# An RWKV-7 block and its experts: k and b side by side in one tile, their products with v and U joined, the slots in another order

## The chip, the cores and the metric

The kernel runs on one core of a Trainium2 chip. The metric is device time in microseconds (us); lower is better. PE is the matrix engine (its weight loads are shown apart, as PEld), DVE the vector engine, ACT the scalar engine, POOL GpSimd, SP the engine that issues most DMAs. "L371" is line 371 of the kernel before.

## What is computed

Sizes: B = 4 batches, H = 8 heads, S = 768 steps, D = 40; then N = 3072 tokens of 320, E = 8 experts of 1024, capacity 80. All float32.

```python
state = zeros(B, H, D, D)
for t in range(S):
    y[:, :, t] = einsum('bhd,bhde->bhe', r_t, state)
    Sa = einsum('bhde,bhe->bhd', state, a_t)
    state = state * w_t[:, :, None, :] - outer(Sa, b_t) + outer(v_t, k_t)
x = y.transpose(0, 2, 1, 3).reshape(B * S, H * D)
logits = x @ w_gate                      # argmax expert, its softmax weight
for e in range(E):                       # at most 80 tokens, by largest weight
    out[tok] = weight[tok, None] * (relu(x[tok] @ w1[e]) @ w2[e])
```

## The kernel before, in words

**Tiling.** The sequence is cut into 12 chunks of T = 64 steps, the batches into two pairs (BP = 2, Z = 2 batches in each), which gives 24 units, in the order chunk 0 pair 0, chunk 0 pair 1, chunk 1 pair 0 and so on. A unit holds 2 batches x 8 heads x 64 steps; partitions are 2 x 64 steps, or, turned, two heads (parity q) x 64 with 40 used. Unit n needs the state that unit n - 2 left.

**What a unit needs.** Within a chunk the recurrence becomes matrix products. decays (L241) turns w with PE transposes and products (L246) takes running products pt with a scan on DVE. decayed_a (L251) makes ahT. inverted (L257) turns pt back with PE, takes its reciprocal on DVE (L265), and POOL multiplies b and k by it (L267, L268) into ub and kh. operand_b and system (L271, L274) turn ub and form the scores N with ahT; the blocks of N go to DRAM. operand_k and psi (L317, L320) do the same for kh: Psi, masked by POOL (L227).

**The inversion.** Four units make a group (NG = 4). fetch (L286) reads the group's 32x32 blocks back, one block per partition; begin (L290) masks them on POOL; 30 steps (L297) of two DVE products each invert the blocks; end (L308) writes them to DRAM and reads them back as dt. Unit n = 4k needs group k's dt.

**A unit's own slot.** right (L343): a first part of PE products from psi and v, a second from the state's copy state_b and ahT; diagonal, below, diagonal (L366, L358) apply the inverse and give u. Then, one slot later (o = n - 1): turned, rT and vT (L382, L327), lower (L391: two sets of scores, copied to lam and masked by POOL), rows (L398, from the turned state gT of reads_g, L332), summed (L409: products with kh and ub), xT and acc on DVE, the new state on POOL (L427), spread (L375: ACT copies the state to state_b). logits (L431) turns xT, writes rows to DRAM and sums the gate's logits; per group, gate (L450) makes weights and keeps running lists of the largest 80 by 10 rounds (L490, L491) on DVE.

**What sets the order.** The order is written out by hand in the loop of L582, and do (L510) chains the instructions of PE, DVE, ACT and POOL in exactly that order; SP's follow their own. Inversion steps and rounds wait in one list, todo; pause(us) (L531) takes from it until the stated costs are used up. PSUM tiles of transposes and small products share the pool ps_t, three buffers (L143); scores have one (L144). Inputs have two buffers each and are loaded two units ahead. Seven units are prepared before the loop (AHEAD = 7, L138), the first inversion among them.

**The end.** The lists are merged, a table of tokens per expert is made, and eight experts are computed; their weights are loaded once the first phase has ended (L648).

Of the kernel before, what the change touches and what calls it, by code (L numbers as in the profile page):

```python
# [18 lines left out]
def kernel(  # L19
# [49 lines left out]

    NF = DM // 128  # L70
    XW = 2 * DM - NF * 128
    assert DM - NF * 128 == 64
    FK = F // 128

    x_dram = nc.dram_tensor("x_rows", (N, XW), F32, kind="Internal")

# [59 lines left out]
    with ExitStack() as p1:  # L136
# [5 lines left out]
        sb = p1.enter_context(tc.tile_pool(name="sb", bufs=2))  # L142
# [8 lines left out]
        def padded(name, n, shape, fill=0.0, where=lambda t: t):  # L151
# [7 lines left out]
        def dims(t):  # L159
            return t[:, :, D:HB]  # L160

        NK = AHEAD + 3
        raw = {n: padded(f"raw_{n}", 2, [128, H, HB], 1.0 if n == "w" else 0.0, dims) for n in inputs}
        decay = padded("decay", 2, [128, G, Z, T + 1], 0.0, lambda t: t[:, :, :, 0:1])
        ubs = padded("ub", NK, [128, H, HB], 0.0, dims)
        khs = padded("kh", NK, [128, H, HB], 0.0, dims)
        us = padded("u", 2, [128, H, HB], 0.0, dims)

        state = padded("state", BP, [128, Z, G, HB], 0.0, lambda t: t)
        state_b = padded("state_b", BP, [128, Z, G, 2, D])  # L170
        og_t = padded("og", 2, [128, NG, 32])
        cand = padded("cand", 2, [128, capr + ZT])

        (lam,) = [hold.tile([128, 2, 2, G, T + D], F32, name="lam")]
# [5 lines left out]
        def load(n, names, queues=(nc.sync, nc.sync)):  # L180
            if n >= NU:
                return
            c, bp = units[n]
            for name in names:
                for z in range(Z):
                    queues[z].dma_start(raw[name][n % 2][halves[z], :, 0:D],
                                        inputs[name][Z * bp + z, :, c * T : (c + 1) * T, :].rearrange("h t d -> t h d"))
# [17 lines left out]
        def copied(name, t, bufs=2):  # L205
            o = sb.tile([128, G, 128], F32, name=name, tag=name, bufs=bufs)
            nc.scalar.copy(o, transposed(t))  # L207
            return o
# [3 lines left out]
        def scores(lhs, rhs):  # L212

            p = ps_s.tile([128, 2, 512], F32, name="sp", tag="s")
            p = p.rearrange("p q (i g t) -> p q i g t", i=2, g=G)
# [14 lines left out]
        def block(z, i):  # L230
            return slice(z * T + i * C, z * T + (i + 1) * C)
# [350 lines left out]
        for n in range(NU + 2):  # L582
# [8 lines left out]
            if past:  # L591
                do(beside, o)
# [242 lines left out]
```

## Time and the profile before

| | |
|---|---|
| median of 3 runs | 674.28 us (668.98 to 681.53) |
| the profiled execution's own time | 669.64 us |
| its span, first to last instruction | 667.9 us |
| mean granted PE clock | 0.912 |
| busy: PE, PEld, DVE, ACT, POOL | 500.3, 434.3, 368.1, 239.0, 197.3 us |
| DMA packets | 224900, of which 205333 under 512 B |
| first copy of a slot (L356) begins | 108.0 us |
| last xT (L421) begins | 537.1 us |

The page gives busy times and what idle time an engine had before a group of instructions, with the one that ended it. It has 40 slices of the span, in which a digit is the busy share in tenths; PEclk is the clock that PE was granted. A timeline row is a run of like instructions: start, length, engine, line, operation, tile written and tiles read, shapes, count. PE executes a float32 product as two instructions, so 16 products are 32 rows' counts; a transpose is one. The loop's slots can be cut at the starts of L356.

### The profile page before, as it was taken

The numbers are of one execution on the slowest core, as the hardware profiler recorded it, in microseconds if no ns is written. First come the engines' busy times: TensorE is split into PE (matmuls) and PEld (weight loads), VectorE is DVE, ScalarE is ACT, GpSimd is POOL, SyncE is SP. The second block draws the span as 40 slices with busy tenths as digits, with TensorE's granted clock in tenths as the row PEclk, the third lists the DMA queues.
The fourth block names the chain that finished last, engine by engine and source line by source line (L and its number), as shares of the span: only waits on it lengthen the run. The fifth ranks groups of instructions, "written<-read, shape, count | busy, mean of one in ns | idle before, by whom it ended". The sixth has DMA issues, their size and how long they took to land. (4 is left out here: it accounts for less than half of the span.)

```text
span 667.9 us, 25885 instructions
## 1 busy us (share of the span) xinstructions
PE 500.3 (75%) x11494; PEld 434.3 (65%) x11494; DVE 368.1 (55%) x851; ACT 239.0 (36%) x500; POOL 197.3 (30%) x273
## 2 busy tenths in 40 slices
PE   3755048798958798886997799769799721799996
PEld 2544037688847688875887688758688620677774
DVE  7525952795349964897659961885150058401110
ACT  1221014455625545553564535554545400000000
POOL 4222012425424424532444433422222200112111
PEclk9999999979978989987998989998989855599999
DMA  8653366535665466545553143123211008999200
GB/s 109 101 108 42 62 117 116 80 60 136 126 149 105 70 149 140 112 94 112 99 115 69 36 97 75 34 75 58 50 19 37 15 12 275 358 318 325 68 7 19
DMA packets 224900, 69.29 MB, mean 104 GB/s; under 512 B 205333, under 2 KB 219797, under 8 KB 224789
## 3 DMA queue, kind: packets, MB, share of 16 engines
q1 hardware_dynamic: 217344, 64.85, 44.1%
q10 hardware_dynamic: 6676, 0.99, 1.1%
q8 instruction: 90, 1.47, 1.0%
q0 software_dynamic: 768, 1.80, 0.9%
q14 instruction: 22, 0.17, 0.1%
HBM read 51.85 MB, written 15.76 MB: 101 GB/s over the span
## 5 line engine op out<-in xcount | busy, mean ns | idle before, releaser
L303 DVE TENSOR_TENSOR tmp<-tt,lt 128x30 f32<-128x30 f32 (+9 forms) x180 | 75.5, 420 | 25.3 <-POOL tt L292 20.5
L306 DVE TENSOR_TENSOR tt<-tt,tmp 128x30 f32<-128x30 f32 (+9 forms) x180 | 79.3, 441 | 6.6
L267 POOL TENSOR_TENSOR ub<-raw_b,ip 128x320 f32<-128x320 f32 x24 | 21.5, 894 | 200.3 <-DVE ip L265 179.6
L227 POOL TENSOR_SCALAR_AFFINE_SELECT lam<-lam 64x1024 f32<-64x1024 f32 x48 | 56.1, 1168 | 71.0 <-ACT lam L395 69.1
L265 DVE RECIPROCAL ip<-pp 128x320 f32<-128x320 f32 x24 | 51.7, 2155 | 37.1 <-PE pp L262 37.1
L421 DVE TENSOR_TENSOR xT<-yp,pt 128x512 f32<-128x512 f32 x24 | 16.5, 687 | 72.8 <-PE yp L417 72.7
L785 ACT ACTIVATE hT<-hp 128x320 f32<-128x320 f32 x16 | 6.1, 434 | 108.7 <-PE hp L781 108.7
L249 DVE TENSOR_TENSOR_SCAN pt<-decay,begins 128x520 f32<-128x520 f32 x24 | 30.0, 1248 | 26.5 <-ACT decay L243 26.5
L262 PE MATMUL pp<-pick,pt 128*64 128x80 f32 x384 | 22.3, 271 | 29.0 <-DVE pt L249 29.0
L417 PE MATMUL yp<-lam,kh 64*64 64x104 f32 (+1 forms) x768 | 29.6, 261 | 16.5 <-POOL lam L227 16.2
L793 DVE TENSOR_SCALAR y<-yp,weight 80x320 f32<-80x320 f32 x8 | 4.4, 547 | 67.6 <-PE yp L791 67.6
L262 PEld LDWEIGHTS pp<-pick,pt 128*64 128x64 f32 x384 | 18.9, 166 | 32.1 <-issue 26.2
L227 POOL TENSOR_SCALAR_AFFINE_SELECT psi<-psi 64x512 f32<-64x512 f32 x48 | 32.2, 672 | 20.2 <-ACT psi L324 18.6
L791 PE MATMUL yp<-w,hT 128*80 128x320 f32 x128 | 37.0, 436 | 0.0
L371 PE MATMUL pr<-yy,dt 32*32 32x40 f32 x1536 | 36.6, 199 | 0.2 <-ACT yy L364 0.2
L371 PEld LDWEIGHTS pr<-yy,dt 32*32 32x32 f32 x1536 | 30.8, 107 | 8.4 <-issue 6.5
L406 PE MATMUL yp<-rT,gT 64*64 64x64 f32 x768 | 35.9, 260 | 0.0
L417 PEld LDWEIGHTS yp<-lam,kh 64*64 64x64 f32 x768 | 22.0, 140 | 21.2 <-POOL lam L227 21.2
L406 PEld LDWEIGHTS yp<-rT,gT 64*64 64x64 f32 x768 | 32.1, 170 | 4.4 <-issue 3.9
L207 ACT COPY ubT<-tp 128x512 f32<-128x512 f32 x24 | 14.1, 586 | 58.1 <-PE tp L202 58.0
L427 POOL TENSOR_TENSOR state<-acc,pt 128x320 f32<-128x320 f32 x22 | 25.0, 1135 | 32.1 <-DVE acc L426 25.1
L395 ACT COPY lam<-sp 128x512 f32<-128x512 f32 x48 | 25.8, 589 | 16.8 <-PE sp L220 16.8
(343 smaller groups left out, 1159.1 us busy)
## 6 DMA issues: line engine op xcount, KB each, us to landing
w<-in_moe_w_dram SPq DMA_DIRECT2D x8, 1280.0 KB, 14.9
w<-in_moe_w_dram SPq DMA_DIRECT2D x8, 1024.0 KB, 16.6
x_rows<-xb SPq DMA_DIRECT2D x48, 96.0 KB, 2.6
out_dram<-zero SPq DMA_DIRECT2D x8, 480.0 KB, 3.6
raw_w<-in_w_dram SPq DMA_DIRECT2D x46, 80.0 KB, 3.0
raw_a<-in_a_dram SPq DMA_DIRECT2D x46, 80.0 KB, 2.8
raw_b<-in_b_dram SPq DMA_DIRECT2D x46, 80.0 KB, 3.0
raw_k<-in_k_dram SPq DMA_DIRECT2D x46, 80.0 KB, 2.9
```

The source lines that it names most:

```text
L227: nc.gpsimd.affine_select(out=oo, in_=oo, compare_op=Alu.is_gt, fill=0.0, base=0, pattern=[[0, oo.shape[1]], [1, T]], channel_multiplier=-1)
L249: nc.vector.tensor_tensor_scan(flat(pt), flat(decay[n % 2]), flat(begins), 0.0, op0=Alu.mult, op1=Alu.add)
L262: nc.tensor.matmul(p[halves[z], g, :], lhsT=pt[:, g, z, 1:], rhs=pick[:, 0, 0 : 2 * D], start=g == 0, stop=True, skip_group_check=True)
L265: nc.vector.reciprocal(ip, p.rearrange("p g (q d) -> p (g q) d", q=2))
L303: nc.vector.tensor_tensor(out=tm, in0=t3[:, 0:i, i : i + 1].to_broadcast([128, i, n]), in1=l3[:, i : i + 1, i + 1 :].to_broadcast([128, i, ...
L306: nc.vector.tensor_tensor(out=t3[:, 0:i, i + 1 :], in0=t3[:, 0:i, i + 1 :], in1=tm, op=Alu.add)
L371: nc.tensor.matmul(o["pr"][m, h, :], lhsT=dt_[m, n % NG, h % 2, h // 2, :], rhs=o["yy"][m, h, :], start=h == 0, stop=True, skip_group_chec ...
L395: nc.scalar.copy(lam[:, :, q, :, 0:T], p[:, q])
L406: nc.tensor.matmul(y[m, z, g, 0:T], lhsT=o["gT"][m, z, g, :], rhs=o["rT"][m, g, halves[z]], start=g == 0, stop=False, skip_group_check=True)
L417: nc.tensor.matmul(o["y"][m, z, g, 0:w_], lhsT=x[halves[z], 2 * g + q, :], rhs=lam[halves[z], i, q, g, 0:w_], start=False, stop=i == 1, sk ...
L427: nc.gpsimd.tensor_tensor(out=st[:, :, :, 0:D], in0=acc, in1=o["pt"][:, :, :, T : T + 1].rearrange("p g z o -> p z g o").to_broadcast([128 ...
L791: nc.tensor.matmul(yp, lhsT=hT[:, f, :], rhs=w2[:, f, :], start=f == 0, stop=f == FK - 1)
```

## The change

- k and b of a batch are loaded onto the two halves of one tile (raw_s): batch 0 has k in partitions 0 to 63 and b in 64 to 127, batch 1 the other way. scaled holds both after the multiplication by inverse decays; u lies beside v in the same manner (side).
- The inverse decays come from a scan backward (backward: a reciprocal of each chunk's last product, then products from the end), not from L265; DVE multiplies (inverted), not POOL.
- operand turns both at once, system forms N and Psi in one set of products whose left side has 128 columns; one copy (system_kept) keeps both, and POOL masks them. lower does the same for v and u. summed has one product where there were two, over all 128 partitions. gT is block diagonal, and rows uses it whole.
- N goes to DRAM whole, in 2 KB rows; fetch takes 32x32 blocks from it with four DMAs.
- Inputs and most tiles of the pool sb have one buffer; SP is chained in order too.
- The loop's order is new. Steps and rounds have lists of their own, with other costs and pauses. x_rows holds 320 values per token, and tokens makes the doubled last 64 with two products.

Its core (turned and system keep their names; `...` marks what is left out):

```diff
-        sb = p1.enter_context(tc.tile_pool(name="sb", bufs=2))
+        sb = p1.enter_context(tc.tile_pool(name="sb", bufs=1))
...
+        raw = {n: filled(f"raw_{n}", i, [128, H, HB], 1.0 if n == "w" else 0.0, lambda t: t[:, :, D:])
+               for n, i in (("w", 1), ("a", 1), ("r", 1))}
...
+        scaled = filled("scaled", NK, [128, Z, H, HB], 0.0, lambda t: t[:, :, :, D:])
+        side = hold.tile([128, 1 + SLOTS, Z, H, HB], F32, name="side")
+        nc.gpsimd.memset(side[:, 1:], 0.0)
...
+        (gT,) = filled("gT", 1, [128, Z, G, 2, HB])
...
+        def by_half(t):
+            ps = [ps_t.tile([128, Z, G, T], F32, name="tp", tag="t") for _ in range(2)]
+            for z in range(Z):
+                for g in range(G):
+                    for p, m in zip(ps, halves):
+                        nc.tensor.transpose(p[:, z, g, :], t[m, z, 2 * g : 2 * g + 2, :].rearrange("p q d -> p (q d)"), ident[m, m])
...
-                            nc.tensor.matmul(p[z, q, i, g, :], lhsT=l[m, g, z], rhs=rhs[m, g, z], start=True, stop=True)
+                    for q, m in enumerate(pars):
+                        nc.tensor.matmul(p[:, q, z, g, :], lhsT=lhs[m, z, g, :], rhs=rhs[m, g, halves[z]],
+                                         start=True, stop=True)
...
+        def backward(n):
+            pt = of[n]["pt"]
+            nc.vector.reciprocal(ends[:, :, :, T:], pt[:, :, :, T:])
+            of[n]["qt"] = qt = sb.tile([128, G, Z, T + 1], F32, name="qt", tag="qt")
+            nc.vector.tensor_tensor_scan(flat(qt)[:, ::-1], decay[n % 2][:, 1:][:, ::-1], flat(ends)[:, ::-1], 0.0,
+                                         op0=Alu.mult, op1=Alu.add)
+        def turned_a(n):
+            of[n]["ap"] = transposed(pairs(raw["a"][0]))
...
-                                           scalar=-1.0, in1=of[n]["pt"][:, :, :, 0:T], op0=Alu.mult, op1=Alu.mult)
...
+            nc.vector.scalar_tensor_tensor(out=by_batch(ahT), in0=by_batch(of[n].pop("ap")), scalar=-1.0,
+                                           in1=of[n]["pt"][:, :, :, 0:T], op0=Alu.mult, op1=Alu.mult)
...
         def inverted(n):
...
+            qt = of[n].pop("qt")
+            of[n]["s"] = s = scaled[n % NK]
+            for z in range(Z):
+                p = ps_t.tile([128, G, 2 * D], F32, name="pp", tag="t")
+                for g in range(G):
+                    for m in halves:
+                        nc.tensor.matmul(p[m, g, :], lhsT=qt[:, g, z, 1:], rhs=pick[:, 0, 0 : 2 * D], start=g == 0,
+                                         stop=True, skip_group_check=True)
+                nc.vector.tensor_tensor(out=s[:, z, :, 0:D], in0=raw["s"][0][:, z].rearrange("p (h d) -> p h d", d=D),
+                                        in1=p.rearrange("p g (q d) -> p (g q) d", d=D), op=Alu.mult)
+            load(n + 1, "s")
...
+        def operand(n):
+            of[n]["sT"] = sT = sb.tile([128, Z, G, 128], F32, name="sT", tag="sT")
+            for p, m in zip(by_half(of[n]["s"]), halves):
+                nc.scalar.copy(sT[:, :, :, m], p)
...
+            o["np"] = scores(o.pop("sT"), o["ahT"])
+        def system_kept(n):
+            o = of[n]
+            p = o.pop("np")
+            o["nt"] = nt = kept.tile([128, Z, 2 * G, T], F32, name="nt", tag="nt", bufs=AHEAD + 1)
+            nc.scalar.copy(nt.rearrange("p z (q g) t -> p q z (g t)", q=2), p.rearrange("p q z g t -> p q z (g t)"))
+            for i, m in enumerate(halves):
+                nc.sync.dma_start(blocks[n // NG, m, n % NG], nt[m, 1 - i])
+            for z, m in enumerate(halves):
+                masked(nt[m, z])
...
+            inverse[k]["lt"] = lt = sb.tile([128, C * C], F32, name="lt", tag="lt")
+            for i in range(Z):
+                for j in range(NS):
+                    m = block(i, j)
+                    nc.sync.dma_start(lt[m].rearrange("p (s t) -> p s t", s=C),
+                                      blocks[k, m, :, :, j * C : (j + 1) * C].rearrange("s u h t -> (u h) s t"))
...
+        def right(n):
+            o, vu, sb_ = of[n], vu_of(n), state_b[units[n][1]]
+            o["pr"] = pr = ps_r.tile([128, H, D], F32, name="pr", tag="r")
+            for h in range(H):
...
+                    nc.tensor.matmul(pr[halves[1 - z], h, :], lhsT=o["nt"][halves[z], z, of_head(n, h), :],
+                                     rhs=vu[halves[z], z, h, 0:D], start=h == 0, stop=False,
+                                     skip_group_check=True)
+            for g in range(G):
+                for z in range(Z):
+                    nc.tensor.matmul(pr[halves[1 - z], 2 * g : 2 * g + 2, :], lhsT=o["ahT"][:, g, halves[z]],
...
+        def beside(n):
+            for i, m in enumerate(halves):
+                nc.scalar.copy(vu_of(n)[m, 1 - i, :, 0:D], of[n]["pr"][m])
...
         def turned(n):
...
+            of[n]["vuT"] = vuT = sb.tile([128, Z, G, 128], F32, name="vuT", tag="vuT")
+            for p, m in zip(by_half(vu_of(n)), halves):
+                nc.scalar.copy(vuT[:, :, :, m], p)
+        def turned_r(n):
+            of[n]["rp"] = transposed(pairs(raw["r"][0]))
+            load(n + 1, "r")
...
+        def reads_r(n):
+            of[n]["rT"] = rT = sb.tile([128, G, ZT], F32, name="rT", tag="rT")
+            nc.scalar.copy(rT, of[n].pop("rp"))
...
-            p = scores((o["vT"], o["uT"]), o["rT"])
...
+            p = scores(o.pop("vuT"), o["rT"])
+            nc.scalar.copy(side[:, 0].rearrange("p z (g q) t -> p q (z g) t", q=2), p.rearrange("p q z g t -> p q (z g) t"))
+            for m in halves:
+                masked(side[m, 0].rearrange("p z h t -> p (z h) t"))
...
                 for g in range(G):
-                    for m in pars:
-                        nc.tensor.matmul(y[m, z, g, 0:T], lhsT=o["gT"][m, z, g, :], rhs=o["rT"][m, g, halves[z]],
-                                         start=g == 0, stop=False, skip_group_check=True)
+                    nc.tensor.matmul(y[:, z, g, 0:T], lhsT=gT[:, z, g, :, :].rearrange("p q e -> p (q e)"),
+                                     rhs=o["rT"][:, g, halves[z]], start=g == 0, stop=False, skip_group_check=True)
...
-            for i, x in enumerate((o["kh"], o["ub"])):
...
-            o["xT"] = xT = sb.tile([128, G, ZT], F32, name="xT", tag="xT", bufs=1)
+                        x = side[:, 0, z, 2 * g + q, :]
+                        if not last:
+                            x = bass.AP(x.tensor, x.offset, [x.ap[0], [(1 + n % SLOTS) * Z * H * HB, 2], [1, HB]])
+                        nc.tensor.matmul(o["y"][m, z, g, 0 : T if last else T + HB], lhsT=o["s"][:, z, 2 * g + q, :], rhs=x,
+                                         start=False, stop=True, skip_group_check=True)
+            if not last:
+                st = own(n)
+                acc = sb.tile([128, Z, G, D], F32, name="acc", tag="acc")
+                nc.vector.tensor_tensor(out=acc, in0=o["y"][:, :, :, T : T + D], in1=st, op=Alu.add)
+                nc.gpsimd.tensor_tensor(
...
+            o["xT"] = xT = sb.tile([128, G, ZT], F32, name="xT", tag="xT")
             nc.vector.tensor_tensor(out=by_batch(xT).rearrange("p g z t -> p z g t"), in0=o["y"][:, :, :, 0:T],
...
-            if not last:
...
-        kinds = [e.engine for e in (nc.tensor, nc.vector, nc.scalar, nc.gpsimd)]
+        kinds = [e.engine for e in (nc.tensor, nc.vector, nc.scalar, nc.gpsimd, nc.sync)]
...
+        def pause(todo, us_):
...
+            steps.extend(((i * (C - 1 - i) * 1.04 + 155) * 2e-3, lambda i=i: step(k, i)) for i in range(1, C - 1))
...
+        def prepare(n):
+            do(backward, n)
+            do(decays, n + 1)
+            do(turned_a, n)
+            do(decayed_a, n)
+            do(forward, n + 1)
+            do(inverted, n)
...
+        def joined(n):
+            do(operand, n)
+            do(system, n)
+            do(system_kept, n)
...
         for n in range(NG):
...
+            prepare(n)
             if n:
...
+                joined(n - 1)
+        joined(NG - 1)
         do(fetch, 0)
...
+        do(load, 0, "rv")
+        prepare(NG)
+        joined(NG)
+        do(load, 1, "v")
+        prepare(NG + 1)
         do(begin, 0)
...
         invert(0)
...
+        pause(steps, 5)
+        joined(NG + 1)
+        do(load, 2, "v")
+        pause(steps, 100)
+        queues[1] = nc.sync
+        prepare(NG + 2)
...
+            if now:
+                do(right, n)
+            if past:
+                do(turned, o)
+            if coming and n:
+                do(system, m)
+            if now:
+                do(diagonal, n, 0)
+            if coming and n:
+                do(system_kept, m)
+                if m % NG == NG - 1:
+                    do(fetch, m // NG)
+            if n == 0:
+                joined(NG + 2)
+                prepare(m)
+                do(operand, m)
+                do(backward, m + 1)
+                do(system, m)
+                do(system_kept, m)
+                do(fetch, m // NG)
+            if past:
+                do(turned_r, o)
+            if next_:
+                do(inverted, m + 1)
+            if past:
+                do(reads_r, o)
+            if now:
+                do(below, n)
+            if past:
+                do(lower, o)
+            if now:
+                do(diagonal, n, 1)
+                do(beside, n)
+            if coming and m % NG == NG - 1:
+                do(begin, m // NG)
+                invert(m // NG)
+            if n % NG == 0:
+                pause(rounds_, 5)
+                pause(steps, 2)
+            else:
+                pause(steps, 3)
+                pause(rounds_, 1.6)
+                pause(steps, 4)
+            if past:
+                do(rows, o)
             if o >= 1:
                 do(logits, o - 1)
...
+                    turn, first_steps, next_steps = gate((o - 1) // NG)
+                    for _, f in first_steps:
+                        do(f)
+                elif (o - 1) % NG == 0 and o - 1 >= NG:
+                    do(turn)
+                    rounds_.extend(next_steps)
+            if next_:
+                do(turned_a, m + 1)
             if now:
                 do(reads_g, n)
...
             if next_:
                 do(decayed_a, m + 1)
+                do(operand, m + 1)
             if past:
                 do(summed, o)
             if far:
+                do(decays, m + 2)
+            if past:
+                do(spread, o)
+            if far:
+                do(forward, m + 2)
+                do(backward, m + 2)
             if 2 <= n < 2 + N // zrows:
                 do(fill, n - 2, n)
+        do(turn)
+        rounds_.extend(next_steps)
+        pause(rounds_, 100)
...
-        for i in range(NF + 1):
+        for i in range(NF):
             nc.tensor.transpose(xp[:, i, :], rows[e][:, i * 128 : (i + 1) * 128], ident[:cap, :cap])
+        for i in range(2):
+            nc.tensor.matmul(xp[64 * i : 64 * i + 64, NF, :], lhsT=rows[e][:, NF * 128 :], rhs=ident[:cap, :cap],
+                             start=True, stop=True, skip_group_check=True)
```

## The prediction

> **What bounds the kernel now.** There is one core, so the first view is the page. Its chain of the work that ended last covers only the last 10 us (output DMAs) and says nothing of the loop. The slices tell more:
>
> ```profile
> PE   3755048798958798886997799769799721799996
> ...
> DVE  7525952795349964897659961885150058401110
> ...
> PEclk9999999979978989987998989998989855599999
> ```
>
> Up to slice 6 is the prologue (before 108.0 us), slices 6 to 31 are the 24 slots of the loop, the rest is routing and experts. In the loop PE is mostly at 8 or 9, DVE swings. So I cut the loop at the starts of the copy of L356 (one per slot) and asked for busy times per stretch; columns: length, then busy PE, PEld, DVE, ACT, POOL, granted clock, DMA.
>
> ```profile
> 241.70:257.30 15.60, 14.71 (x458) 13.52 (x456) 9.64 (x24) 9.43 (x21) 7.40 (x9) 1.00 0.69 134
> 257.30:273.10 15.80, 14.71 (x458) 13.40 (x454) 8.39 (x17) 9.62 (x20) 8.89 (x11) 1.00 0.61 127
> 273.10:293.30 20.20, 16.73 (x458) 15.01 (x456) 19.33 (x36) 9.82 (x20) 8.11 (x9) 0.92 0.55 118
> 293.30:316.70 23.40, 17.28 (x459) 15.48 (x457) 19.41 (x49) 9.89 (x21) 7.34 (x9) 0.85 0.44 90
> ```
>
> These are slots 7 to 10. Two of a group of four are PE's (14.7 of 15.7 us), two are DVE's (19.4 busy), where PE waits and its clock falls. A group is 75.0 us; slots 1 to 15 together 287.7, slots 16 to 22 110.6. What one PE burst costs I read from weight-load rows of the timeline at full clock (start, length, count last):
>
> ```profile
> 323.32 0.56 PEld L220 LDWEIGHTS sp<-ahT,khT 64*64 64x64 f32 x32
> ...
> 326.61 0.97 PEld L437 LDWEIGHTS xp__5010<-pick,xT 128*128 128x128 f32 x8 [1.36 <-DVE xT L421]
> ...
> 328.10 1.00 PEld L406 LDWEIGHTS yp<-rT,gT 64*64 64x64 f32 x31 [0.17 <-issue]
> ...
> 331.49 0.61 PEld L353 LDWEIGHTS pr<-state_b,ahT 128*64 128x64 f32 x16
> ...
> 607.80 0.97 PEld L781 LDWEIGHTS hp<-xe,w1b 64*128 64x128 f32 x16
> ```
>
> 32 loads of 64*64 tiles cost 0.56 us where four quarters of the array alternate (L220), 1.00 where two do (L406). A 64*128 load, two alternating, costs 0.97/16 = 61 ns, a 128*128 one 121 ns. DVE's inversion steps depend on what POOL does:
>
> ```profile
> 69.32 0.40 DVE L303 TENSOR_TENSOR tmp<-tt,lt 128x228 f32<-128x228 f32 x1
> ...
> 426.24 1.21 DVE L303 TENSOR_TENSOR tmp<-tt,lt 128x228 f32<-128x228 f32 x1
> ```
>
> The second ran under a POOL mask of 64x1024. The nearest row for the new fetch, 128 KB in 128-byte pieces, is in the list of DMA issues (last column: us to landing):
>
> ```profile
> dt<-solved SPq DMA_DIRECT2D x24, 128.0 KB, 3.2
> ```
>
> **What the Trainium skill says.** "TensorE: Matmul & The Clock Gate", LDWEIGHTS: a load costs by its columns, not by the contraction rows. The trace agrees: 64*128 and 128*128 are 122 and 121 ns per row half. Same page, Part 1: an idle window of about 3.4 us halves the clock; here half-clock stretches follow DVE's slots (0.85 in slot 10). "GPSIMD Engine Reference", Key points: GpSimd contends with DVE instructions that have two SBUF inputs; 1.21 against 0.40 agrees. "TensorEngine Tiling (Array Packing)", Key Properties: a new tiling mode drains the array; bursts here stand 0.1 to 0.2 us apart, which the rows below leave room for.
>
> **PE, per slot.** Removed: four scores bursts ub, kh, v, u on four quarters (0.60 + 3 x 0.56 = 2.28), four transposes of 4 (0.47 + 0.47 + 0.42 + 0.42 = 1.78), inverted 0.63, rows 1.00, summed 0.75 + 1.05 = 1.80. Together 7.5. Added: system and lower, 32 loads of 64*128 each (2 x 1.94); turned and operand, 16 transposes of 64*128 each (2 x 0.97); inverted doubled, 1.26; rows, 16 loads of 128*128, 1.94; summed, 32 of 128*64 with 128 columns moving instead of 80: 2 x 0.61 x 128/80 = 1.95. Together 11.0. The array holds fewer instructions (452 to 372 by the code's counts) but each fills 128 columns where a quarter did. Balance +3.5; a row counts its last load's latency, so +2.3 to +3.5. Unchanged: right 1.62, both diagonals 1.28, below 0.73, r, a, w 1.36, logits 0.97, reads_g 1.02, so the new slot holds 6.98 + 11.0 = 17.9 of PE.
>
> **DVE, ACT, POOL.** DVE loses L265 (2.16) and gains the second scan (1.23 as the first; its reversed steps are in no trace, 1.0 to 2.5, I take 1.25: it runs in DVE's idle 3 us before the next products and costs nothing up to there), a reciprocal of 8 elements (0.18 to 0.2, from L475's 178 ns) and two products out of PSUM (2 x 0.48 as L426): 5.45 becomes 5.7 per slot. POOL loses ub, kh and the copy of xb (2.0 us); its masks of 512 and 1024 stay. POOL's state product was 1.53 us under the scan and 0.74 without; acc now comes before xT (one PSUM input), so 0.74. ACT stays near 10 us, under PE, and costs nothing unless the slot falls below that. Memsets at the start and the pad products are hidden under the first loads.
>
> **The wait that is new.** In the new order the slot's DVE queue is: two products of inverted, steps and rounds (S), logits' reduce, ahT, acc, xT, two scans. logits, turned_a and reads_g hold all three ps_t buffers; operand needs two, so it waits for the reduce, which stands behind S. Behind operand on PE stand summed, decays and the next right; behind these the next inverted, for which DVE waits. So S and PE are in series. The circle, from the end of right's second part: turned 0.97, system 1.94, diagonal 0.64, r 0.47, first half of inverted 0.63, handover 0.3, two products 0.96, S, reduce 0.18, operand 0.97, summed 1.95, handover 0.3, acc 0.48, state 0.74, spread 0.93, three handovers 0.3, second part of right 0.61: 12.4 + S. State to spread to right used to have half a slot of room; now right follows at once, so even without S PE stalls 2.75 - 0.47 - 1.01 = 1.3 us, and a slot is at least 17.9 + 1.3 - 0.4 (latency counted twice) = 18.8.
>
> S follows from the pauses and the steps' stated costs, which steps 6 to 11 of the prologue exceed by 1.11 (4.67 us against 4.21), plus 1.7 us where they run under POOL's masks (2.3 + 0.6 us overlapped, of which 0.6 is lost). By n mod 4:
> 1: steps 6 to 16, 9.1 + 1.7, and from n = 9 one round 0.9: 11.7, slot 24.1 (23.2 before).
> 2: steps 17 to 26, 8.0 + 1.7: slot 22.1.
> 3: four steps and two rounds, 4.1: slot 18.8, PE's.
> 0: begin waits for the fetch in the same slot, which is now four DMAs of 128-byte pieces: nt ready 5.3, two issues 1.3, landing 2.2, three issues at 0.83, landing 3.2, mask and memset 1.4, so 15.9; five steps 2.65, then the circle's rest 6.5: slot 25.1. SP does these in order; r, s and x_rows queue behind, with a slot's time to spare.
> Slots 1 to 3: 64.1; 4 to 7: 89.2; 8 to 15: 180.2. Sum 333.5, against 287.7: +46. PE now idles 4 to 6 us in three of four slots, so the clock falls about as often or more; +0 to +20, I take +4. Together +50.
>
> **The rest.** Slots 17 to 22 have no system, operand or inverted: 12.9 of PE and a stall of 1.7, 14.6 each; slot 16, whose reduce waits for the fetch, 21.5. Sum 109, -1.5; the drain +2. Prologue: PE is cold there (L202's four transposes take 1.1 us, 0.6 later). A unit took 7.24 us; now 6.6 at full clock and 10.6 at half (system alone 3.4); but the first fetch had slack behind POOL, and slot 0 now holds two units that stood ahead of it: -10 to +15, I take +4. Single raw buffers: each load has a slot, 3 us needed. Experts: one expert's tokens gain three small products, +0.1 each; the loads still wait for the end of phase one: +0.5.
>
> Sum: 669.6 + 50 + 0.5 + 4 + 0.5 = 725 in the frame of the profiled execution (span 667.9, 1.7 around it); the median shown is 4.6 above it, so 730.
>
> **Rivals.** (A, 0.52) As above, 705 to 765. (B, 0.17, the other side) S stays hidden: the scheduler finds operand its buffers without the reduce, and slots are PE's alone at 17.5 (no state stall): 15 x 17.5 = 262, -25, rest as above: 655, at best 645. It decides once 12.4 + S is below 17.5, S below 5; for it speak the even pauses, against it that reduce is traced after them. With the stall kept, 18.8 x 15 = 282 gives 674. (C, 0.18) Series, but the fetch and contention cost nothing: slots of 21.2, 22.4, 20.4 and 18.8 by n mod 4, those before the rounds lighter, 306 for the 15, +18: 690 to 705. (D, 0.13) Series, and every idle gap halves the clock for another 3.4 to 7 us of PE work: some 2 us more in each of 15 slots, and the prologue cold, +15: 765 to 790. That the new program does not do what it says is not a case: the counts follow from the code.
>
> **Numbers.** About 2% is what a measurement of this kernel tells from no change. B gives faster 0.12 and same 0.05, C the rest of same, 0.03; A, D and most of C are slower: 0.80. Range 667 to 768: it leaves B's lower half and D's upper half out. A alone: 705 to 765.
>
> **What would show it.** Scores rows of 32 at about 1.9 us and rows at 1.9 bear out PE; PE waiting at operand's transposes for DVE's reduce, and DVE at the two products for PE, the series; right's second part behind spread the stall; the first step of n mod 4 = 0 behind POOL's tt near 16 us into the slot the fetch. Slots alike at 18 us, with operand not waiting, would make it wrong; so would 64*128 loads near 30 ns.

## The result, and the profile after

The changed kernel takes 787.22 us (median of 4 runs, 778.20 to 801.04) against 671.63 before (median of 4 in the same comparison, 667.91 to 681.53). Executions of both kernels fall into faster and slower ones; the ratio of the faster ones alone is 1.163 (95% interval 1.151 to 1.175; the ratios below are of this kind), and the profiled execution is one of the slower (801.04 us, span 799.1), so its stages are some 14 us longer together than the median's. The forecast was slower, at 730 us with 768 as its upper end; the sign is right, the size is not.

From here on L is a line of the kernel after: L244 scores, L233 by_half, L303 and L305 the products of inverted, L351 and L354 the steps, L374 and L379 the two parts of right, L447 rows, L460 summed, L465 acc, L478 spread, L486 and L490 logits and its reduce.

The slices of the page after, three rows of 40, answer to those of before:

```profile
PE   4885389889688797787976978799989980499997
...
DVE  8326723773275545754467535543310148600000
...
PEclk9655555999798898978999979869696555567999
```

DVE no longer alternates between 4 and 9 in the loop; it is nowhere above 8. PE is busy as before or more, and late in the loop (slices 26 to 31) PEclk shows 5 or 6 in four slices of six, where it was 8 or 9. At the start of the experts both kernels have three 5s, and the changed one a 6 and a 7 behind them. In the prologue the row of before misleads: its record of the granted clock begins only at 106.5 us, and before its first entry the row reads 9. The bursts of the prologue ran at half clock before the change too, the same 16 loads taking 1.13 us there and 0.63 at its end (view of before):

```profile
96.06 1.13 PEld L262 LDWEIGHTS pp<-pick,pt 128*64 128x64 f32 x16 [2.01 <-issue]
...
107.70 0.63 PEld L262 LDWEIGHTS pp<-pick,pt 128*64 128x64 f32 x16
```

So the mean of 0.912 before is too high, and the prologue is no place where only the changed kernel is slow.

Busy time by stretch, cut at the copy behind right (L382); columns as before (length, PE, PEld, DVE, ACT, POOL, clock, DMA). Slots 5 to 8, then 17 and 18:

```profile
224.28:250.78 26.50, 20.64 (x374) 18.66 (x376) 17.60 (x42) 9.67 (x19) 5.02 (x7) 0.87 0.35 74
250.78:276.88 26.10, 20.31 (x376) 18.58 (x377) 15.11 (x30) 9.66 (x18) 5.72 (x6) 0.87 0.36 76
276.88:296.15 19.27, 17.82 (x374) 16.26 (x376) 9.26 (x25) 9.66 (x18) 5.67 (x6) 1.00 0.57 131
296.15:322.65 26.50, 20.62 (x375) 18.64 (x376) 13.33 (x41) 9.66 (x18) 6.16 (x8) 0.87 0.58 111
513.95:536.39 22.44, 21.06 (x286) 19.57 (x288) 11.55 (x37) 7.51 (x15) 3.26 (x4) 0.60 0.13 24
536.39:551.12 14.73, 13.08 (x287) 11.97 (x289) 8.59 (x27) 6.99 (x14) 3.01 (x3) 1.00 0.19 36
```

In the loop three slots of a group of four take 26 us, one 19.3 with PE busy almost throughout. Slots 17 and 18 hold the same PE instructions (286 and 287); one takes 14.7 us at full clock, the other 22.4 at 0.60. The weight-load rows of these two slots say what that is (start, length):

```profile
512.57 1.10 PEld L379 LDWEIGHTS pr<-state_b,ahT 128*64 128x64 f32 x16 [5.09 <-ACT state_b L478]
...
518.34 3.49 PEld L244 LDWEIGHTS sp<-rT,vuT 64*128 64x128 f32 x32
...
523.15 3.49 PEld L447 LDWEIGHTS yp<-rT,gT 128*128 128x128 f32 x16
...
539.18 1.86 PEld L244 LDWEIGHTS sp<-rT,vuT 64*128 64x128 f32 x32
...
541.80 1.86 PEld L447 LDWEIGHTS yp<-rT,gT 128*128 128x128 f32 x16
...
545.83 1.73 PEld L460 LDWEIGHTS yp<-side,scaled 128*64 128x64 f32 x32
```

After one wait of 5 us PE works without a gap from 512.6 to 532, yet at half clock: 3.49 us for bursts that take 1.86 a slot later. A much shorter wait can be enough. Slots 19 and 20 begin behind like waits of some 1.5 us; the clock stays in one and falls in the other:

```profile
550.30 0.61 PEld L379 LDWEIGHTS pr<-state_b,ahT 128*64 128x64 f32 x16 [1.56 <-ACT state_b L478]
...
553.90 1.86 PEld L244 LDWEIGHTS sp<-rT,vuT 64*128 64x128 f32 x32
...
564.92 0.61 PEld L379 LDWEIGHTS pr<-state_b,ahT 128*64 128x64 f32 x16 [1.57 <-ACT state_b L478]
...
569.79 3.49 PEld L244 LDWEIGHTS sp<-rT,vuT 64*128 64x128 f32 x32
```

The wait in the loop, slot 5, in the timeline of DVE and PE:

```profile
228.70 1.04 DVE L305 TENSOR_TENSOR scaled<-raw_s,pp 128x320 f32<-128x320 f32 x2 [3.24 <-PE pp L303]
...
240.69 0.18 DVE L490 TENSOR_REDUCE lg<-xp__2659 128x8 f32<-128x32 f32 x1
...
240.93 0.27 PE L233 MATMUL tp<-ident,scaled 64*128 64x64 f32 x1 [4.05 <-DVE lg L490]
...
243.74 3.68 PE L460 MATMUL yp<-side,scaled 128*64 128x128 f32 x32
...
247.54 0.49 DVE L465 TENSOR_TENSOR acc<-yp,state 128x320 f32<-128x320 f32 x1 [4.00 <-PE yp L460]
```

This is the forecast's circle, link by link: DVE waits for PE's products, PE at operand for DVE's reduce behind the steps, DVE for summed. But summed takes 3.68 us, not the 1.95 it was costed at. By stage, in the profiled executions (us; the names are those of the experiments below):

| | before | forecast | after | n1 narrow | n3 no steps | n5 split | n9 held | n11 fitted |
|---|---|---|---|---|---|---|---|---|
| prologue and slot 0 | 119.0 | 123.0 | 130.8 | 114.1 | 104.1 | 122.8 | 129.2 | 110.5 |
| slots 1 to 15 | 287.7 | 337.5 | 362.3 | 359.9 | 291.0 | 328.3 | 361.6 | 283.6 |
| slots 16 to 22 | 110.6 | 109.0 | 132.4 | 110.9 | 118.7 | 118.7 | 117.3 | 100.8 |
| slot 23 and drain | 20.4 | 22.4 | 31.5 | 20.3 | 27.4 | 27.4 | 20.3 | 18.1 |
| lists and experts | 130.2 | 130.7 | 142.1 | 132.4 | 141.2 | 141.3 | 132.6 | 135.7 |
| span | 667.9 | 722.6 | 799.1 | 737.5 | 682.3 | 738.4 | 761.0 | 648.6 |

### The profile page after: what moved, and what is told of

It reads as the page before. It is cut to its first block, busy times and chain, and to the rows that moved or that the text cites. A ratio compares the mean times of both kernels' runs of the same rounds, so it can differ in the third digit from the quotient of the medians.

```text
span 799.1 us, 22012 instructions
## 1 busy us (share of the span) xinstructions
PE 630.5 (79%) x9598; PEld 561.0 (70%) x9598; DVE 359.1 (45%) x914; ACT 239.4 (30%) x452; POOL 142.7 (18%) x184
## 3 DMA queue, kind: packets, MB, share of 16 engines
q10 hardware_dynamic: 11428, 1.73, 1.4%
## 5 line engine op out<-in xcount | busy, mean ns | idle before, releaser
L351 DVE TENSOR_TENSOR tmp<-tt,lt 128x30 f32<-128x30 f32 (+9 forms) x180 | 70.2, 390 | 42.4 <-POOL tt L340 37.0
L250 POOL TENSOR_SCALAR_AFFINE_SELECT side<-side 64x1024 f32<-64x1024 f32 x48 | 55.1, 1147 | 129.6 <-ACT side L436 128.3
L354 DVE TENSOR_TENSOR tt<-tt,tmp 128x30 f32<-128x30 f32 (+9 forms) x180 | 66.8, 371 | 6.6
L244 PE MATMUL sp<-ahT,sT 64*128 64x64 f32 x768 | 59.6, 318 | 11.1 <-ACT sT L312 11.1
L250 POOL TENSOR_SCALAR_AFFINE_SELECT nt<-nt 64x512 f32<-64x512 f32 x48 | 31.5, 656 | 199.0 <-ACT nt L322 197.8
L244 PEld LDWEIGHTS sp<-ahT,sT 64*128 64x128 f32 x768 | 56.9, 231 | 12.3 <-ACT sT L312 12.3
L460 PE MATMUL yp<-side,scaled 128*64 128x128 f32 (+1 forms) x768 | 63.8, 339 | 0.0
L233 PE MATMUL tp<-ident,scaled 64*128 64x64 f32 x384 | 27.8, 282 | 44.8 <-DVE lg L490 28.3
L460 PEld LDWEIGHTS yp<-side,scaled 128*64 128x64 f32 x768 | 57.3, 182 | 2.4 <-issue 0.2
L233 PEld LDWEIGHTS tp<-ident,scaled 64*128 64x128 f32 x384 | 21.4, 182 | 50.1 <-DVE lg L490 29.3
L244 PE MATMUL sp<-rT,vuT 64*128 64x64 f32 x768 | 55.1, 301 | 1.8 <-ACT rT L431 1.8
L447 PE MATMUL yp<-rT,gT 128*128 128x64 f32 x384 | 56.3, 308 | 0.0
L303 PE MATMUL pp<-pick,qt 128*64 128x80 f32 x768 | 39.8, 267 | 19.1 <-DVE qt L283 17.3
L244 PEld LDWEIGHTS sp<-rT,vuT 64*128 64x128 f32 x768 | 51.5, 212 | 3.4 <-ACT rT L431 2.1
L447 PEld LDWEIGHTS yp<-rT,gT 128*128 128x128 f32 x384 | 52.8, 220 | 1.5
L303 PEld LDWEIGHTS pp<-pick,qt 128*64 128x64 f32 x768 | 35.2, 164 | 24.9 <-issue 19.8
L305 DVE TENSOR_TENSOR scaled<-raw_s,pp 128x320 f32<-128x320 f32 x48 | 22.8, 482 | 65.0 <-PE pp L303 64.1
L465 DVE TENSOR_TENSOR acc<-yp,state 128x320 f32<-128x320 f32 x22 | 10.8, 490 | 76.3 <-PE yp L460 76.3
L379 PE MATMUL pr<-state_b,ahT 128*64 128x80 f32 x384 | 20.8, 257 | 26.6 <-ACT state_b L478 26.6
## 6 DMA issues: line engine op xcount, KB each, us to landing
w<-in_moe_w_dram SPq DMA_DIRECT2D x8, 1280.0 KB, 14.6
```

The source lines that it names most:

```text
L233: nc.tensor.transpose(p[:, z, g, :], t[m, z, 2 * g : 2 * g + 2, :].rearrange("p q d -> p (q d)"), ident[m, m])
L244: nc.tensor.matmul(p[:, q, z, g, :], lhsT=lhs[m, z, g, :], rhs=rhs[m, g, halves[z]], start=True, stop=True)
L250: nc.gpsimd.affine_select(out=o, in_=o, compare_op=Alu.is_gt, fill=0.0, base=0, pattern=[[0, o.shape[1]], [1, T]], channel_multiplier=-1)
L303: nc.tensor.matmul(p[m, g, :], lhsT=qt[:, g, z, 1:], rhs=pick[:, 0, 0 : 2 * D], start=g == 0, stop=True, skip_group_check=True)
L305: nc.vector.tensor_tensor(out=s[:, z, :, 0:D], in0=raw["s"][0][:, z].rearrange("p (h d) -> p h d", d=D), in1=p.rearrange("p g (q d) -> p ( ...
L351: nc.vector.tensor_tensor(out=tm, in0=t3[:, 0:i, i : i + 1].to_broadcast([128, i, n]), in1=l3[:, i : i + 1, i + 1 :].to_broadcast([128, i, ...
```

## The experiments

Two theories stood at the start. The circle: the series through DVE is longer than costed. The clock: the wide tiles do not keep, and do not bring back, PE's full clock. Each kernel is the changed one with the edit shown.

**n1, the same products in narrow tiles.**

```diff
-  nc.tensor.matmul(p[:, q, z, g, :], lhsT=lhs[m, z, g, :], rhs=rhs[m, g, halves[z]], ...)
+  for c in halves:
+      nc.tensor.matmul(p[c, q, z, g, :], lhsT=lhs[m, z, g, c], rhs=rhs[m, g, halves[z]], ...)
...
-  nc.tensor.matmul(y[:, z, g, 0:T], lhsT=gT[:, z, g, :, :]..., rhs=o["rT"][:, g, halves[z]], ...)
+  for q, m in enumerate(pars):
+      nc.tensor.matmul(y[m, z, g, 0:T], lhsT=gT[m, z, g, q, :], rhs=o["rT"][m, g, halves[z]], ...)
```

> The same arithmetic in narrower tiles: each 64*128 product of system and lower as two of 64*64 on the four quarters (64 instructions at about 17.5 ns instead of 32 at 54), and rows on two diagonal quarters (32 at 31 ns instead of 16 at 111). At full clock PE falls by 2 x 0.6 + 0.8 = 2.0 us per slot. Clock theory (what the forecast missed is half-clock time, because wide tiles spend half their time on weight loads and do not bring the full clock back): the slots of 22.4 us after the system has run out (17, 20, 22) vanish, slots 16 to 22 fall from 132 to about 90 to 95 us, the drain from 31 to 20, and the total to 680 to 715. Circle theory (the series through DVE is longer than costed, the clock is a by-product): only 0.6 us of the 2.0 lies in the circle of the slots that DVE's steps bind; the late slots keep their 22.4 us; total 745 to 765.

Measured 739.18 us (ratio to before 1.104, 1.094 to 1.113): neither total. Slots 16 to 22, the drain and the experts fall to about what they were before the change and the prologue below it, which leans to the clock theory; but slots 16 to 22 were to take 90 to 95 and take 110.9, and there and in the drain the clock still falls four times, for 7 to 14 us each. Against n3 and n5, which keep the wide tiles and take 118.7 in these slots, that is 7.8 us, and the 1.4 us less that PE has to do in each of them (13.2 against 14.6 at full clock) would explain it. So n1 alone does not separate the tiles' clock from their cost. Slots 1 to 15 stay at 359.9, with more half clock than with the wide tiles (112 us against 80), although PE has some 2 us less to do in each: there something else than PE's work binds. A late slot at full clock, weight loads of n1:

```profile
526.18 1.02 PEld L245 LDWEIGHTS sp<-rT,vuT 64*64 64x64 f32 x64
...
528.00 1.01 PEld L449 LDWEIGHTS yp<-rT,gT 64*64 64x64 f32 x32
```

Twice as many instructions, 1.02 and 1.01 us instead of 1.86 and 1.86.

**n2, the reduce ahead of the steps.** The lines of logits, turned_a and decayed_a are moved from behind the pauses to ahead of them; nothing else.

> logits with its reduce, turned_a and ahT are put ahead of the pauses with the inversion's steps, so that operand's ps_t buffers come free before the steps. Circle theory: operand and summed (2.4 us with the reduce and a handover) leave the circle, which is now products, steps, acc, state, spread, right, inverted: about 3 us less in each of the 11 slots of 1 to 15 with more than 6 us of steps, total 745 to 755, PE no longer waits at operand for DVE's reduce. Clock theory: besides, PE idles in shorter pieces, 10 to 20 us more, total 730 to 740; the slots 17, 20 and 22 stay at 22 us in both. If operand waits for something else than these buffers: 780 to 790.

Measured 833.90 us (1.232, 1.213 to 1.252): slower than the change itself; both theories had the sign wrong. The timeline of slot 6 shows where the wait went:

```profile
271.79 0.19 DVE L490 TENSOR_REDUCE lg<-xp__2954 128x8 f32<-128x32 f32 x1 [4.70 <-ACT xb L489]
...
284.86 1.34 PE L379 MATMUL pr<-state_b,ahT 128*64 128x80 f32 x16 [4.73 <-ACT state_b L478]
```

operand no longer waits. But the reduce needs logits, which stands late in PE's order, so the steps start 4.7 us later than the products allow; and acc still stands behind them, so the wait goes to right, through acc, state and spread. What has to leave the circle is the steps, not the reduce.

**n3, no inversion steps.** The line that lists the steps (L582) is left out.

> The inversion's steps (two DVE instructions each) are left out, so the inverse is only the initial matrix; everything else runs. It prices S. Circle theory: slots 1 to 15 fall to 18.8 to 19.5 us each, together 285 to 295 instead of 362. Clock theory for the late part: slots 17, 20 and 22 have no steps of their own and stay at about 22 us, 16 to 22 about 125. Together 695 to 715. If fetch or POOL bound the slots instead of DVE's steps, n mod 4 = 0 keeps over 23 us.

Measured 684.03 us (one run; before 676.06). Slots 1 to 15 take 291.0, inside the 285 to 295 expected, at clock 0.99, and those of n mod 4 = 0 18.4 each: without steps the fetch binds nothing. So 71 us of these slots come from the steps standing in series, the half clock behind the waits included. Among the late slots two long ones remain (23.1 and 22.1), and the experts take 141.2: the steps have no part in those. Three long ones were in the profile after, in other places; n5 has the same two as n3.

**n4b, tile shapes by themselves.** A kernel of eight bursts, each of one shape, one behind the other (one run).

> Computes nothing of the reference: after gaps of some 25 us without PE work, bursts of fp32 products of one tile shape each, about 25 us long at half clock, each row half on a PSUM bank of its own. In order: 64*128 with 64 columns moving (system, lower); 128*128 with 64 (rows); 128*64 with 128 (summed); 64*64 with 64 on four quarters; the same on two diagonal quarters; 64*128 with 128; 128*128 with 128; 128*64 with 64. Clock theory: the first two stay at half clock to their end (102 and 210 ns per instruction), the third and fourth return to full clock within two windows of 3.4 us, so do the sixth and seventh, which load the same columns as the first two but move twice as many. Rival (PE's busy time decides): all eight return after one or two windows.

The gaps came out at 0.4 to 9 us, not 25, but the first burst begins cold and leaves the second cold. Groups of four of the bursts (busy us and mean ns of one; pipelined, so the pitch is busy time over count):

```profile
L43 PE MATMUL sa<-x,left 64*128 64x64 f32 x512 | 54.9, 418 | 5.2 <-ACT left L35 5.2
L43 PE MATMUL sb<-x,left 128*128 128x64 f32 x256 | 54.9, 421 | 0.6 <-ACT left L35 0.6
L43 PE MATMUL sc<-x,left 128*64 128x128 f32 x512 | 30.6, 286 | 0.4 <-ACT left L35 0.4
...
L43 PE MATMUL sf<-x,left 64*128 64x128 f32 x384 | 24.3, 292 | 4.9 <-ACT left L35 4.9
```

sa runs at 54.9 / 512 = 107 ns and sb at 214, start to end: twice the 54 to 56 ns of L244 at full clock, and nearly twice the 115 of L447. The clock never came back in 55 us of unbroken work each, and the record of the granted clock has its first rise at 120.8 us, in sc. sc ran 5 us at 107 ns, then at 55. sf loads the same columns as sa and moves twice as many: 112 ns for 5 us, then 56. So at nearly equal pitch twice the columns go through; with 64 of them the pitch is, by this, the weight load's, and the columns themselves would need about half of it. PE's busy time does not tell the two apart (both count 100%), so for these bursts the rival falls. That sa and sb came first in the program does not explain it: in the profile after, the record has the clock at full from 13.2 us on, for 6.8 us. The other shapes do not contradict: 64*64 on two quarters (53, later 29 ns) and 128*128 with 128 moving (112 ns) returned within 4 us; four quarters and 128*64 with 64 began at full clock and tell nothing of the return.

**n5, the last pause behind the scans.**

```diff
             if n % NG == 0:
                 pause(rounds_, 5)
-                pause(steps, 2)
             else:
                 pause(steps, 3)
                 pause(rounds_, 1.6)
-                pause(steps, 4)
...
                 do(backward, m + 2)
+            pause(steps, 2 if n % NG == 0 else 4)
```

> Only the last pause of each slot (4 us of steps, 2 where n mod 4 = 0) is moved, from ahead of rows to behind the two scans, where DVE otherwise waits 4 to 9 us for the next inverted; the order of the steps stays. Series theory (S stands between products and operand, so it adds to the slot): S in the circle falls from 4 to 11 us to 2 to 6, all slots become PE's at 18.5 to 20 us, slots 1 to 15 together 285 to 305 instead of 362, clock there above 0.95; what is not the series stays (slots 16 to 22 near 132, drain 31, tail 142 in the profiled execution): 705 to 730 in all. If the moved steps only make the next products late: slots of 22 to 24, 330 for the 15, 750 to 760.

Measured 745.31 us (1.116, 1.111 to 1.121). Slots 1 to 15 gain 34 us, half of what was expected. Seven slots take 18.4 to 19.8 as expected; those of 21 to 28 are not the series any more. In slot 7:

```profile
254.60 1.09 PE L303 MATMUL pp<-pick,qt 128*64 128x80 f32 x16 [1.54 <-DVE scaled L305]
...
256.83 3.68 PE L244 MATMUL sp<-rT,vuT 64*128 64x64 f32 x32
...
261.65 3.67 PE L447 MATMUL yp<-rT,gT 128*128 128x64 f32 x16
```

The moved steps make DVE's products late, and PE waits 1.5 us for one; from then on it waits for nothing long and still needs 3.68 and 3.67 us for lower and rows. Here too the clock fell behind a wait of 1.5 us.

**n6 and n7, split and narrow together; turned between the parts of right.** n6 is n1 with n5's edit; n7 also puts turned (PE 0.6 us) ahead of right's second part.

> The moved pause and the narrow tiles of the first experiment together. If the two causes are separate and add up (series: some 65 us in slots 1 to 15; wide tiles and their clock: some 50 us in the prologue, the late slots, the drain and the tail), the narrow tiles now count in the loop too, since PE binds it: slots of 16.5 to 18, 250 to 270 for the 15, 635 to 655 in all, below the kernel before. If the series is only replaced by another one (state, spread, right): slots stay at 19 and the total is 665 to 680.

> The sixth kernel with the second part of right moved behind the transposes of turned, so that PE has 0.5 us of work while acc, state and spread run. If PE stalls 1.3 us per slot there, 0.5 to 0.7 us less in each of some 22 slots: 10 to 15 us below the sixth kernel. If the stall is covered already: no difference (within 1%).

n6: 696.47 us (before 670.20); n7: 689.66 (1.033, 1.026 to 1.041). The gains add, but slots 1 to 15 take 308 and 305, not 250 to 270: from slot 6 on those of n mod 4 = 2 and 3 take 22 to 24, since 4 us of steps make PE wait up to 3.5 us for DVE's products, and those of 0 and 1 17 to 21. n7 is 7 us below n6; the runs of n7 spread by 13 us and those of n6 by 19, so that gain is not settled. In slots 1 to 15 half clock lasts 5.3 us at a time in n6 (3.4 to 10.2) and 10.8 in n5 (3.4 to 17.1), which have the same steps behind the scans. But the narrow tiles are no cure: among n6's late slots one stretch lasts 17.1 us, and its experts take 139.7, n7's 143.8.

**n9, products of zeros that nobody reads.** The changed kernel with, between the parts of right, in spare columns of right's PSUM bank:

```diff
+            for _ in range(10):
+                nc.tensor.matmul(bank[:, H * D : 512], lhsT=still[:, 0:128], rhs=still[:, 0 : 512 - H * D],
+                                 start=False, stop=True, skip_group_check=True)
...
     tokens(0)
+    keep_at_work(ps_y, "y", 10)
```

> The changed kernel with nothing taken away, only products of zeros added that nobody reads: ten of 128*128 in bf16 with 192 columns (0.8 us at full clock) between the two parts of right, where PE waits for the state, and ten with 256 behind the first expert's transposes. Clock theory (the late slots, the drain and the experts are long because the clock stays at half, not because of the number or cost of their products): slots 16 to 22 fall from 132 in the profiled execution (119 in another kernel with the same late slots) to 103 to 110, the drain from 31 to 20 to 24, the tail from 142 to 130 to 133; slots 1 to 15 lose little, since the series remains: 745 to 765 in all. Cost theory (the wide products themselves are what is long): 0.8 us more in each slot, 795 to 810.

Measured 760.91 us (1.135, 1.128 to 1.142, where the change has 1.163): some 19 us faster than the change by these ratios, by adding work. Slot 22 and slot 23 with the drain, first in the profile after, then in n9:

```profile
602.69:625.46 22.77, 21.32 (x287) 19.69 (x289) 3.11 (x10) 7.19 (x14) 3.01 (x3) 0.60 0.08 17
625.46:656.90 31.44, 29.61 (x344) 27.62 (x344) 7.34 (x26) 9.37 (x17) 4.56 (x4) 0.55 0.08 16
...
593.40:608.10 14.70, 13.98 (x297) 12.71 (x298) 3.11 (x10) 7.00 (x14) 3.02 (x3) 1.00 0.12 25
608.10:628.40 20.30, 17.51 (x344) 16.08 (x344) 7.34 (x26) 9.09 (x17) 4.57 (x4) 1.00 0.12 26
```

Both at full clock: 22.8 has become 14.7, 31.5 has become 20.3, the experts 132.6. A slot like 22 can stay at full clock without the products (15.1 in n3, 15.0 in n5), so the better measure is the rest: slots 18 to 22 all at full, the drain 20.3 where n3 and n5 have 27.4, the experts 132.6 where they have 141.2 and 141.3. Slot 17 (22.2), behind a wait of 4.7 us, was not held, and slot 16 took 21.6, so 117.3 missed the 103 to 110 and is hardly below the 118.7 of n3 and n5. The cost theory, with 0.8 us more per slot, is out.

**n8, n10, n11, n12: fitting the steps to the waits.** n8 is n7 with the pieces 2 us behind the products, 2 behind ahT, 3 behind the scans; n10 adds n9's products (eight per slot); n11 moves the gate's small instructions behind operand and the rounds behind ahT, and takes 2.5, 2 (n mod 4 = 2 only) and 2.5 us of steps; n12 is n11 without the products in the slots.

> The seventh kernel (narrow tiles, turned between the parts of right) with the steps spread over three stretches in which DVE waits: 2 us of them behind the products, 2 behind ahT (while PE runs operand and summed), 3 behind the scans, 4 where n mod 4 = 0. In the seventh the slots of n mod 4 = 2 and 3 were 22.6 to 24 and those of 0 and 1 16.8 to 18.6. If the pieces now fit the waits: all slots 16.5 to 18, slots 1 to 15 together 255 to 270 instead of 305, 640 to 660 in all, below the kernel before. If acc is delayed instead by the piece behind ahT, state, spread and right follow late: 680 to 695, no gain.

> The eighth kernel with the added products of zeros of the ninth (eight per slot instead of ten). If the clock at the experts' start and after the short waits in the slots is what is left: 10 us less in the tail (142 to 131) and 5 to 15 in the slots, together 15 to 25 below the eighth. If PE is already at full clock in the slots: only the tail gains, and the slots lose up to 0.6 us each.

> The tenth kernel with the pieces of DVE's work fitted to the waits its trace shows: the gate's ten small instructions and their Exp go behind operand (they stood ahead of ahT and delayed gT's copy by 1.5 us), the lists' rounds behind ahT instead of ahead of the reduce, 2.5 us of steps instead of 2 behind the products, 2.5 instead of 3 behind the scans (3 us made the next products 2 us late in n mod 4 = 3). If DVE's queue is what still holds PE: slots 1 to 15 fall from 295 to 260 to 275 in the profiled execution and the whole to 640 to 660, 2 to 4% below the kernel before. If the clock alone is left (0.92 there): 665 to 675, no change.

> The eleventh kernel without the eight added products per slot (those behind the first expert's transposes stay). If they keep the clock in the slots: 5 to 15 us above the eleventh, and half-clock stretches return in the late slots. If nothing falls to half clock there any more: 5 to 10 us below it, since their 0.8 us per slot is saved only where PE does not wait for the state.

n8: 678.22 us (1.013, 1.008 to 1.019); n10: 674.14 (1.010, 1.002 to 1.018), its tail 7.5 and its late slots 10 us shorter than n8's, its slots 1 to 15 4 us longer; n11: 654.48 against 676.24 before (0.970, 0.960 to 0.979), so about 3% faster than the kernel before, with runs from 648 to 667 against 667 to 679; n12: 656.28 (0.971, 0.962 to 0.979), not told apart from n11. So most of the deficit comes back with the order of DVE's work, once the tiles are narrow; n8's slots were not all 16.5 to 18 as expected (290 us for the 15, n11 284 at clock 0.93).

## Why the prediction was right or wrong

- **PE's prices: right at full clock.** scores 1.86 us (1.94 forecast), rows 1.86 (1.94), summed 1.73 (1.95); only the new transposes cost 0.57, not 0.97. The PE-bound slot is 19.3, forecast 18.8.
- **The circle and S: right.** From the products' end to the reduce 11.0 to 11.6 us where n mod 4 = 1 (11.7) and 9.8 where it is 2 (9.7); from the reduce to the next slot 6.9 at full clock (6.5 by the forecast's terms). n3 prices the whole at 71 us.
- **The fetch: right.** tt is ready 14.9 to 17.2 us into the slots 4, 8 and 12 (15.9); these take 24.9 to 27.9 (25.1). Without steps behind it (n3) it costs little.
- **State to spread to right: right.** The waits of the page after:

```profile
PE pr L379 <- ACT state_b L478: 26.6, 22, 5.0
```

26.6 us in 22 slots: one of 5.0, the others 1.0 on average (1.3). The state product takes 0.74 as forecast.
- **The clock: the step that failed.** "so the clock falls about as often or more; +0 to +20, I take +4", and with it the late slots at "14.6 each", "the drain +2" and the experts' "+0.5". The count was right: in slots 1 to 15 the clock fell 8 times before and 10 times after. What was mis-sized is how long PE then stays at half, 48 us of these slots before and 80 after, and in the late slots and the drain, 22 before and 84 after. In the profiled execution the surplus over the forecast is 7.8 us in the prologue and slot 0, 24.8 in slots 1 to 15, 23.4 in 16 to 22, 9.1 in the drain and 11.4 at the end, 76.5 in all. In the loop it sits between the reduce and the next slot: 7.4 to 11.6 us in ten of slots 2 to 15, and 6.9 in the four where n mod 4 = 3; the surplus over 6.9 is 26 us together. The late slots that kept the clock took 14.5 to 14.7, as forecast; n9 shows that in the drain and the experts it is the clock and not the products. How many late slots lose it differs: n3 and n5, with the same instructions there, have 48 us of half clock instead of 84 and are only 9.7 over the forecast in slots 16 to 22 and 5.0 in the drain.
- **What I had overlooked.** The clock was treated as falling with long idle time and coming back with busy time. It fell behind waits of 1.4 to 1.5 us as well: of six such waits for the state (1.4 to 1.8 us on PE, before slots 18 to 23) three were followed by half clock and three were not, and no run here shows what decides. And busy time did not always bring it back. In the Trainium skill, "TensorE: Matmul & The Clock Gate", Part 1, one busy window of some 3.4 us is enough for that; in the loop of the kernel before, each window in which PE had no gap did bring it back. Measured here, 55 us of work did not (sa, sb), so for these shapes the measurement decides. From slot 2 to the drain of the profile after the clock came back 14 times, each time in a window of 3.4 us with summed in it (128 columns moving on a load of 64), and never in one filled by lower or rows. In the loop the wait stands just ahead of summed, so half clock lasts 3 to 10 us; in the late slots it stands ahead of diagonal, lower and rows, and lasts 17 to 20. The loads' width was in the forecast as a price of PE time only; n4b shows that it is also a price in clock. Inside the kernel this is in part argued: in n3 and n5 the clock also came back in windows filled by logits and reads_g without summed, and in n1 two windows full of narrow products left it at half.
- **The rivals.** D named the right end of the scale (765 to 790) by half the mechanism: it had the idle gaps of the 15 slots and the prologue, but 3.4 to 7 us for each gap, and nothing in the late slots or the experts. For the loop it was near: 24.8 us over the forecast, where it had about 30. That the total fell into its range is in part luck, since the late slots, the drain and the experts, which it left out, made up the rest. B is out: n3 shows that S was not hidden. So is C: the fetch and the contention cost what was forecast.

What stays open: how much of the prologue's 7.8 us is the clock and how much its order (n1 takes 16.7 off both together); why the experts' clock falls a second time, which narrow tiles stopped in n1 and not in n6 and n7, so that the 11.4 us there are not shown to come from the tiles; and why n10 gained nothing over n8 in slots 1 to 15.

## What to carry to other kernels

Price a wide stationary tile twice: by its load, and by whether enough columns move over it to bring PE's clock back; sf moved twice the columns of sa at nearly the same pitch, and only sf came back to full clock. When two engines meet twice in a slot, look for the work that stands between the meetings on one of them, and move that work, not the instruction that waits. A stage that waits only 1.5 us per slot can lose 8 us of it when the clock falls (14.6 against 22.4), so look at short stalls too.

## What was not expected of the hardware

- A float32 product with a 64*128 or 128*128 stationary tile and 64 columns moving ran at half clock for 55 us without a break (107 and 214 ns per instruction, n4b); with 128 columns moving over the same 64*128 load the full clock was back after 5 us.
- A wait of some 1.5 us was enough for the clock to fall, in three of six cases in the late slots of the profile after.
- Two 64*64 products on four quarters cost 1.02 us per 64 instructions; one 64*128 in their place costs 1.86 per 32.
- 0.8 us per slot of products of zeros held the full clock in n9 from slot 18 to the drain (slots 14.5 to 15.0 us, where without them those that lost it took 22.4 and 22.8), and did not behind a wait of 4.7 us.
